# Half tails over the whole array width, and the last batch's fourth product by blocks of tokens

## The chip, the core and the metric

The kernel runs on one core of one Trainium2 chip. The metric is the device time of one execution in microseconds, smaller is better. The kernel before takes 279.53 us (median of three executions, 279.29 to 279.78).

The core's engines each follow their own instruction stream in order. PE multiplies matrices (PEld is its weight load, which runs beside the multiplication), DVE and ACT work elementwise, POOL here only starts DMA loads that convert float32 to bfloat16, and SP starts DMA stores and DMA transposes. PE writes to PSUM, eight banks of 128 partitions by 512 float32 each; DVE and ACT read them.

## The reference

Eight batches of eight heads, 576 tokens, 64 dimensions each: attention in a window of 128 tokens with a linear bias, then a token mixer and a channel MLP on the 512 joined columns.

```
scores = scale * q @ k^T ; bias = -slope[h] * |rel| ; kept where 0 <= rel < 128
x   = softmax(scores + bias) @ v            # [8, 576, 512] with the heads side by side
u   = x + (relu(x^T @ w_tok1) @ w_tok2)^T   # over tokens
out = u + relu(u @ w_ch1) @ w_ch2           # over channels
```

## The kernel before, in words

**Planner.** The kernel does not issue instructions as it walks its loops. Each piece of work is an operation with an engine, a cost in ns, a rank, its inputs and its buffers (`plan.op`, L76). `Plan.run` (L118) plays all of them through on paper: at each step it takes, over all engines, the operation that can start earliest, ties going to the lower rank. `Plan.emit` writes the instructions in the order of the planned starts. So a changed cost can change the order on every engine. Among the costs of PE stands a `mode`: where an operation's mode differs from that of the one before it, the planner adds 95 ns (L267). Random shifts of the ranks have fixed seeds for each batch (L337).

**Stages.** For each batch there is a `side` (L873): attention by blocks of 128 tokens, then the token mixer. And there is a `main` (L993): the channel MLP. The side of batch b+1 is planned to run among the main of batch b. On PE, a block's scores are L670; the exponential on ACT is L693; the multiplication by the window's mask on DVE is L703; the product with V is L736, in two groups of four heads (even heads, odd heads); the division by the row sums is L749 and L752 on DVE (L758 when it falls to ACT). V carries a column of ones, so a product has 65 columns, 64 sums and the row sum.

**Token mixer.** L781 and L791 are its first product, L799 or L800 its ReLU, L824 and L820 its second product, L842 on DVE the addition that gives `ub`. From batch 2 on, SP transposes `ub` by DMA into `uT` (L850); before that PE does it (L859).

**Channel MLP.** L1021 is the first product, in chunks of four matmuls of 512 columns; L1064 is the same for the tail. The second product is a scheme of seven half products in `second` (L1135): products 1, 5, 6, 2, 3, 7, 4 in that order, 12 matmuls of 256 columns each (L1198), in two groups of six. On PE's rows they show by their operands: `WC,r` are products 1 and 2, `WT,s` products 5 and 6, `WC,s` product 3, `WT,r` products 7 and 4. Products 1, 6, 7 and 4 add up in one bank, `g2`, with an addition on DVE (L1169) after each of them. The four finished quarters of the result (256 tokens by 256 columns, 256 KB) go out on SP (L1181), or on POOL in the middle batches. L1109 is the second product of the tail, L1116 its addition, L1126 its store. The last batch has another form of the first product (`unit`, L943 to L987).

**Tails.** 576 tokens are four blocks of 128 and a tail of 64. The tails of two batches share one block of 128 rows, `TAIL`. In the first two pairs (batches 0 to 3; `HALVED`, L345) each batch works out its own half: its 64 tokens are 64 weight columns of the product with V, which land on 64 of PSUM's partitions. In the last two pairs both halves are done at once. A half's operation carries `mode=2`; scores carry `mode=1`.

**End.** The last PE work is product 4 of batch 7, then one addition on DVE of 128 partitions by 512, then one store of 256 KB on SP:

```
L1189  4: (1, 0, True)      # quarter: lower 256 tokens, left 256 columns; last, so it is stored
L1197  first = g == 0 and c == 0 and t == 0 and m not in AFTER
L1198  pe_.matmul(bk()[:, c * HN : (c + 1) * HN], lhsT=l(t, c), rhs=w(t), start=first, ...
```

The 12 matmuls are issued as two groups of six: three of the six steps of the sum for tokens 256 to 383 (`c` = 0) and the same three for tokens 384 to 511 (`c` = 1), then the other three steps of each.

Of the kernel before, what the change touches and what calls it, by code (L numbers as in the profile page):

```python
# [11 lines left out]
ALU = mybir.AluOpType  # L12
# [53 lines left out]
class Plan:  # L66
# [51 lines left out]
    def run(self):  # L118
# [28 lines left out]
        mode, turned = 0, -1e9  # L147
# [53 lines left out]
        def send(o, at, line, work, late):  # L201
            nonlocal flying
            coming.append([at, line, work, o, late])
            flying += 1

        while todo:
            best = None
            for e, c in cand.items():
                pick, early = None, None
                for o in c:  # L210
                    if e == "POOL" and o is not pool[sent]:
                        continue
                    t = max(ready[o], free[e])
# [6 lines left out]
                    for b in o.bufs:  # L220
                        if b.slot is None:
                            got = b.ring.best(b.choice, asked.count(b.choice))
                            asked.append(b.choice)
                            if got is None:
                                t = None
                                break
                            t = max(t, got[0])
                    if t is None:
                        continue
                    if e == "POOL" and len(lanes) >= 8:  # L230
                        if lanes[-8].done is None:
                            continue
                        t = max(t, lanes[-8].done)
# [26 lines left out]
            if e == "PE":  # L260
                slow = 2.0 if t < WARM else 1.0
                if t > free[e] + 1.0:
                    self.gaps.append((free[e], t))
                    if t > free[e] + 3000:
                        slow = 1.6
                    t += 60.0
                elif o.mode != mode:  # L267
                    t += 95.0
                mode = o.mode
                o.t0 = t  # L270
                free[e] = t + o.cost * slow
                o.done = free[e] + 165.0
            elif e == "ACT":
                o.t0, free[e], o.done = t, t + o.cost - 115, t + o.cost
            elif e == "DVE":
                o.t0, free[e], o.done = t, t + max(o.cost - 80, 50), t + o.cost
            elif e == "SP":
                o.t0 = t
                if o.bus:
                    free[e] = t + 1310.0  # L280
                    if o.bus > 1500 and len(turns) > 1:
                        free[e] = max(free[e], turns[-2].done + 1100)
                    turns.append(o)
                    send(o, t + 300, 1, TURN[o.bus > 1500][0], TURN[o.bus > 1500][1])
                else:
                    free[e] = t + 590
                    send(o, t + 300, 1, STORE, 1010.0)
            else:
                o.t0 = t
                free[e] = t + o.cost  # L290
                send(o, t + o.cost, 0, STORE if o.packets < 0 else o.packets * PACKET, 1010.0 if o.packets < 0 else LATE[t > FETCH])
                lanes.append(o)
                sent += 1
# [63 lines left out]
STORE = 774.0  # L357
# [11 lines left out]
def kernel(  # L369
# [15 lines left out]
    nc = tc.nc  # L385
    P = nc.NUM_PARTITIONS
    B, H, S, D = q.shape
    DTOK = moe_w_tok1.shape[1]
    DM = H * D
# [30 lines left out]
    def bank(choice=ONE):  # L420
        return plan.buf("ps", choice)
# [171 lines left out]
    for e in range(2):  # L593
        def go(e=e):
            for i in range(2):
                dve_.tensor_copy(out=maskt[:, e, :, 0, i * R : (i + 1) * R], in_=masks[:, e, :, 0, 0:R])
            dve_.tensor_copy(out=maskt[:, e, :, 1, :], in_=masks[:, e, :, 1, :])
            dve_.memset(maskt[0:R, e, :, 1, R:P], 0.0)
# [112 lines left out]
    def values(pr, blk, half, pb, rank):  # L711
        xb = xbs[pr]
        tail = blk == TAIL
        r0, r1_ = (0, P) if half is None else (half * R, (half + 1) * R)
        vme = held[pr, blk]["v"]
        work = [(r0, r1_, 1, vme)]
        if tail:
            work += [(j * R, (j + 1) * R, 0, held[pr, (j + 1) * NC - 1]["v"]) for j in range(2)
                     if half is None or half == j]
        elif blk % NC:  # L720
            work += [(0, P, 0, held[pr, blk - 1]["v"])]
        both = pr >= PAIRN
        ot = None
        for es in ([[0, 1]] if both else [[0], [1]]):
            n = len(es)
            ot, rt = plan.buf("ps", TWICE) if both else bank(), plan.buf("rt")

            def view(ot=ot, n=n):
                v = ot().rearrange("p (e c) -> p e c", e=n)[:, :, 0 : 4 * (D + 1)]
                return v.rearrange("p e (i d) -> p e i d", i=4)  # L730

            for at, e in enumerate(es):
                def go(e=e, at=at, view=view):
                    mms = [(a, z, kind, vb, i, h) for a, z, kind, vb in work for i, h in enumerate(HEADS[e])]
                    for m, (a, z, kind, vb, i, h) in enumerate(mms):
                        pe_.matmul(view()[a:z, at, i, :], lhsT=pb()[:, e, i, kind, a:z], rhs=vb()[:, h, 0 : D + 1],  # L736
                                   start=m == 0, stop=m == len(mms) - 1, skip_group_check=True)

                rk = rank(240)
                plan.op("PE", 120 * len(work) + (110 if tail and half is None else 0), go, rk,  # L740
                        mode=2 if half is not None else 0, reads=[(pb, e)], uses=[w[3] for w in work],
                        **({"adds": ot} if at else {"makes": ot}))

            def x4(es=es):
                v = xb()[r0:r1_, blk, :].rearrange("p (i e d) -> p e i d", i=4, e=2)
                return v[:, es[0] : es[-1] + 1, :, :]

            def recip(view=view, rt=rt, n=n):
                dve_.reciprocal(out=rt()[r0:r1_, 0:n, :, :], in_=view()[r0:r1_, :, :, D : D + 1])  # L749

            def norm(view=view, rt=rt, n=n, x4=x4):
                dve_.tensor_tensor(out=x4(), in0=view()[r0:r1_, :, :, 0:D],  # L752
                                   in1=rt()[r0:r1_, 0:n, :, :].broadcast_to([r1_ - r0, n, 4, D]), op=ALU.mult)

            def norms(view=view, rt=rt, n=n, x4=x4):
                for e in range(n):
                    for i in range(4):
                        act_.activation(out=x4()[:, e, i, :], in_=view()[r0:r1_, e, i, 0:D], func=ACT.Copy,  # L758
                                        scale=rt()[r0:r1_, e, i, :])

            plan.op("DVE", 180 + 4 * (n - 1), recip, rk, makes=rt, uses=[ot])
            plan.op("DVE", 154 + 270 * n, norm, rk, part=(xb, (blk, half)), uses=[ot, rt],
                    other=("ACT", 115 + 830 * n, norms))
# [370 lines left out]

    def second(b, rank, r2, ss, sums, ub):  # L1135
        pr, half = b // 2, b % 2
        g1, g2, g3 = bank(ANY), bank(ANY), bank(ANY)
        obs = {}
        capt = {}

# [15 lines left out]
        BANK = {1: g2, 6: g2, 7: g2, 4: g2, 2: g1, 5: g3, 3: g3}  # L1156
        AFTER = {6: 1, 7: 6, 4: 7, 3: 5}

        def evict(m, bk, row, col, last):
            key = (row, col)  # L1160
            blks = [half * NC + 2 * row, half * NC + 2 * row + 1]
            cols = slice(col * HN, (col + 1) * HN)
            old = obs.get(key)
            ob = old or obs.setdefault(key, plan.buf("ob"))

            def go():
                v = ob().rearrange("p (c n) -> p c n", c=2)
                src = v if old else ub()[:, blks[0] : blks[0] + 2, cols]
                dve_.tensor_tensor(out=v, in0=bk().rearrange("p (c n) -> p c n", c=2), in1=src, op=ALU.add)  # L1169

            rk = rank(0)
            kw = {"adds": ob} if old else {"makes": ob, "reads": [(ub, x) for x in blks]}
            kw["uses"] = [bk]
            capt[m] = plan.op("DVE", 690, go, rk, **kw)
            if not last:
                return
            late = FROM_P <= b < B - 1
            q_ = nc.gpsimd if late else nc.sync

            def store():  # L1180
                q_.dma_start(out=out[b, row * HS : (row + 1) * HS, cols].rearrange("(c p) n -> p c n", p=P),  # L1181
                             in_=ob().rearrange("p (c n) -> p c n", c=2))

            if late:
                plan.dma(store, 2 * P, -1, uses=ob)
            else:
                plan.op("SP", 550, store, rk, uses=[ob])

        DONE = {1: (0, 0, False), 5: (1, 1, False), 6: (0, 1, False), 7: (1, 1, True), 2: (0, 0, True), 3: (0, 1, True), 4: (1, 0, True)}  # L1189
        for m in PRODUCTS:  # L1190
            l, w, s, tt = L[m]
            bk = BANK[m]
            for g in range(2):
                def go(m=m, g=g, l=l, w=w, bk=bk):
                    for c in range(2):
                        for t in range(3 * g, 3 * g + 3):
                            first = g == 0 and c == 0 and t == 0 and m not in AFTER  # L1197
                            pe_.matmul(bk()[:, c * HN : (c + 1) * HN], lhsT=l(t, c), rhs=w(t), start=first,  # L1198
                                       stop=g == 1 and t == HK - 1, skip_group_check=True)

                rd, needs = [], []
# [14 lines left out]
                if SECOND_LATE and g == 0 and m not in AFTER:  # L1216
                    marks["wait"].append(op)
            evict(m, bk, *DONE[m])

    def along(base, length, total):  # L1220
        done = [0.0]
# [68 lines left out]
```

## Time and profile before

| | us |
|---|---|
| median of three executions | 279.53 |
| the profiled execution, its own time | 280.54 |
| its span, first to last instruction | 278.6 |
| outside of the span | 1.94 |
| PE busy | 271.4 |
| DVE busy | 208.0 |
| ACT busy | 136.0 |
| POOL busy | 116.0 |

The granted clock of PE is 0.997 of full over the span. A line of the timeline reads: start in us from the span's start, duration in us, engine, source line, operation, output<-inputs, the array tile in use (rows*columns), output partitions x columns, and how many instructions were merged into the line; at its end, in brackets, how long the engine had stood idle and what ended that. The duration of a PE line includes the last matmul's way through the array, so the pace is read from start to start. The lines themselves stand in the prediction.

### The profile page before, as it was taken

How to read it: one execution, taken by the hardware profiler on the slowest of the kernel's cores; microseconds unless marked ns; L12 is line 12 of the kernel's file. 1: busy time of each engine (PE TensorE's matmuls, PEld its weight loads, DVE VectorE, ACT ScalarE, POOL GpSimd, SP SyncE). 2: the span in 40 equal slices, each digit the busy share in tenths (PEclk: the TensorE clock that was granted, in tenths of full speed). 3: DMA queues.
4: the chain of work that ended last, by engine and by line, in shares of the span. 5: the costliest groups of instructions: out<-in, count | busy, mean ns of one | idle time of the engine just before them, and what ended most of it. 6: DMA issues, size and time to landing. Idle time of an engine off the chain costs nothing.

```text
span 278.6 us, 6964 instructions
## 1 busy us (share of the span) xinstructions
PE 271.4 (97%) x2825; PEld 180.0 (65%) x2825; DVE 208.0 (75%) x485; ACT 136.0 (49%) x219; POOL 116.0 (42%) x146
## 2 busy tenths in 40 slices
PE   7999999999999999999999999999999999999994
PEld 3664765675686556585567655486667645689883
DVE  7566689978897559862989479673989549876982
ACT  5561885336960189206961097206870079205610
POOL 8999765940256027900486009700472220013000
PEclk9999999999999999999999999999999999999998
DMA  9999999999899999999999979999499750043014
GB/s 133 155 138 152 182 190 192 155 125 203 141 113 100 172 251 123 123 142 180 182 133 158 205 191 88 148 138 240 69 115 99 197 142 2 2 118 129 0 53 137
DMA packets 167535, 38.43 MB, mean 138 GB/s; under 512 B 155792, under 2 KB 166672, under 8 KB 167504
## 3 DMA queue, kind: packets, MB, share of 16 engines
q0 software_dynamic: 116112, 20.03, 92.8%
q1 hardware_dynamic: 50352, 17.70, 32.9%
q8 instruction: 22, 0.36, 0.6%
q10 hardware_dynamic: 1040, 0.26, 0.4%
q14 instruction: 9, 0.07, 0.1%
HBM read 35.85 MB, written 9.44 MB: 163 GB/s over the span
## 4 chain that ended last, share of the span: by engine, by line
PE 85%; DMA 6%; POOL 3%; DVE 2%; issue 1%; ACT 1%; SPq 0%; POOLq 0%
PE ps L1198 25%; PE ps L1021 25%; PE ps L736 6%; PE ps L670 5%; PE ps L824 5%; PE ps L781 5%; PE ps L1064 4%; PE ps L943 3%; PE ps L1109 3%; POOL qk L515 3%; DMA qk<-in_k_dram 2%; DMA qk<-in_q_dram 2%; DMA uT<-ub 1%; PE ps L630 1%; PE ps L791 1%
## 5 line engine op out<-in xcount | busy, mean ns | idle before, releaser
L1021 PE MATMUL ps<-uT,WC 128*128 128x512 bf16 x328 | 79.3, 379 | 0.8 <-DMA uT<-ub 0.7
L693 ACT ACTIVATE pe<-ps 128x1024 bf16<-128x1024 f32 (+1 forms) x76 | 63.4, 888 | 30.4 <-PE ps L670 30.1
L515 POOL DMA_DIRECT2D v<-in_v_dram x40 | 34.0, 860 | 92.8 <-PE ps L736 89.0
L1027 ACT ACTIVATE r<-ps 128x512 bf16<-128x512 f32 x75 | 44.4, 601 | 41.4 <-PE ps L1021 39.6
L1021 PEld LDWEIGHTS <-WC 128*128 128x128 bf16 x328 | 29.1, 98 | 31.1 <-issue 2.3
L703 DVE TENSOR_TENSOR pe<-pe,mask 128x1024 bf16<-128x1024 bf16 (+1 forms) x64 | 38.1, 608 | 9.0 <-ACT pe L693 8.5
L1198 PEld LDWEIGHTS <-r 128*128 128x128 bf16 x384 | 37.1, 98 | 7.3 <-issue 0.2
L515 POOL DMA_DIRECT2D qk<-in_k_dram x39 | 33.8, 873 | 2.9 <-DMA v<-in_v_dram 1.4
L515 POOL DMA_DIRECT2D qk<-in_q_dram x39 | 33.5, 864 | 2.4 <-DMA WC<-in_moe_w_ch_dram 1.3
L1198 PEld LDWEIGHTS <-s 128*128 128x128 bf16 x288 | 27.5, 98 | 5.9 <-issue 1.3
L752 DVE TENSOR_TENSOR xb<-ps,rt 128x256 bf16<-128x256 f32 (+1 forms) x72 | 29.0, 416 | 0.7
L736 PEld LDWEIGHTS <-pe 128*128 128x128 bf16 (+1 forms) x560 | 22.4, 100 | 9.2 <-DVE pe L703 2.1
L736 PE MATMUL ps<-v,pe 128*128 128x65 bf16 (+1 forms) x560 | 26.5, 194 | 0.1
L1198 PE MATMUL ps<-WC,r 128*128 128x256 bf16 x192 | 25.4, 273 | 0.0
L1198 PE MATMUL ps<-WT,s 128*128 128x256 bf16 x192 | 24.6, 273 | 0.0
L1198 PE MATMUL ps<-WT,r 128*128 128x256 bf16 x192 | 23.9, 273 | 0.0
L1169 DVE TENSOR_TENSOR ob<-ps,ub 128x512 f32<-128x512 f32 x22 | 15.0, 685 | 10.3 <-PE ps L1198 10.1
L842 DVE TENSOR_TENSOR ub<-ps,xb 128x512 bf16<-128x512 f32 x34 | 21.2, 681 | 1.9 <-PE ps L824 1.8
L670 PEld LDWEIGHTS <-qkT 64*128 64x128 bf16 x560 | 14.8, 94 | 11.2 <-issue 9.8
L670 PE MATMUL ps<-qkT 64*128 64x128 bf16 (+1 forms) x304 | 19.4, 216 | 0.0
L749 DVE RECIPROCAL rt<-ps 128x4 f32<-128x4 f32 (+1 forms) x76 | 12.4, 175 | 8.8 <-PE ps L736 8.2
L1069 ACT ACTIVATE r2t<-ps 128x512 bf16<-128x512 f32 x12 | 7.2, 602 | 22.5 <-PE ps L1064 22.5
(95 smaller groups left out, 340.1 us busy)
## 6 DMA issues: line engine op xcount, KB each, us to landing
out_dram<-ob SPq DMA_DIRECT2D x17, 256.0 KB, 2.6
v<-in_v_dram POOLq DMA_DIRECT2D x32, 128.0 KB, 5.3
qk<-in_k_dram POOLq DMA_DIRECT2D x31, 128.0 KB, 5.5
qk<-in_q_dram POOLq DMA_DIRECT2D x31, 128.0 KB, 5.0
WC<-in_moe_w_ch_dram POOLq DMA_DIRECT2D x8, 384.0 KB, 9.1
out_dram<-raw SPq DMA_DIRECT2D x7, 256.0 KB, 2.8
out_dram<-ob POOLq DMA_DIRECT2D x5, 256.0 KB, 3.4
out_dram<-raw POOLq DMA_DIRECT2D x3, 256.0 KB, 2.9
```

The source lines that it names most:

```text
L515: nc.gpsimd.dma_start(out=to()[p0 : p0 + n, :, :], in_=rows(src, b, s0, n))
L670: pe_.matmul(wide(e)[:, i, kind, a:z], lhsT=ts[kb]()[e * D : (e + 1) * D, NHP + i, :], rhs=ts[blk]()[e * D : (e + 1) * D, i, a:z], start=n ...
L693: act_.activation(out=pb()[:, e, :, lo:, c0:c1_], in_=wide(e)[:, :, lo:, c0:c1_], func=ACT.Exp, scale=scale)
L703: dve_.tensor_tensor(out=o, in0=o, in1=heads(mk, es), op=ALU.mult)
L736: pe_.matmul(view()[a:z, at, i, :], lhsT=pb()[:, e, i, kind, a:z], rhs=vb()[:, h, 0 : D + 1], start=m == 0, stop=m == len(mms) - 1, skip_g ...
L752: dve_.tensor_tensor(out=x4(), in0=view()[r0:r1_, :, :, 0:D], in1=rt()[r0:r1_, 0:n, :, :].broadcast_to([r1_ - r0, n, 4, D]), op=ALU.mult)
L781: pe_.matmul(t1[j]()[:, :], lhsT=W1[:, c, j * P : (j + 1) * P], rhs=xb()[:, blk, :], start=c == 0, stop=False)
L842: plan.op("DVE", 690, lambda blk=blk, ht=ht, hs=hs: dve_.tensor_tensor(out=ub()[:, blk, :], in0=ht()[:, hs], in1=xb()[:, blk, :], op=ALU.a ...
L1021: pe_.matmul(ct()[:, :], lhsT=WC1[:, cb, t * P : (t + 1) * P], rhs=uT()[:, cb, :], start=cb == 0, stop=cb == NCB - 1)
L1027: plan.op("ACT", 600, lambda t=t, ct=ct: act_.activation(out=r2()[:, t, :], in_=ct()[:, :], func=ACT.Relu), rk, part=(r2, t), uses=[ct], o ...
L1169: dve_.tensor_tensor(out=v, in0=bk().rearrange("p (c n) -> p c n", c=2), in1=src, op=ALU.add)
L1198: pe_.matmul(bk()[:, c * HN : (c + 1) * HN], lhsT=l(t, c), rhs=w(t), start=first, stop=g == 1 and t == HK - 1, skip_group_check=True)
```

## The change

In the planner's cost of a store on SP, a store that is given a smaller cost than 550 takes a smaller share of the queue. Beyond that there are two edits of the work.

First, the half tails' product with V (batches 0 to 3) uses all 128 weight columns and writes all 128 partitions; the 64 rows that are not of this half are never read. The operation loses `mode=2`. The number of matmuls stays the same.

Second, in batch 7 `g2` is a pair of neighbouring banks, the first 256 columns of each in use: tokens 256 to 383 (and 0 to 127) in the one, the others in the second. Product 4 of this batch is issued by `last_product`: six matmuls for tokens 256 to 383, their addition of 128 by 256, a store of 128 KB on SP, and the same for tokens 384 to 511 with the store on ACT's queue.

```diff
@@ Plan.run
-                    send(o, t + 300, 1, STORE, 1010.0)
+                    send(o, t + 300, 1, STORE * o.cost / 550, 1010.0)
@@ values
-                    mms = [(a, z, kind, vb, i, h) for a, z, kind, vb in work for i, h in enumerate(HEADS[e])]
+                    mms = [(0 if half is not None else a, P if half is not None else z, kind, vb, i, h)
+                           for a, z, kind, vb in work for i, h in enumerate(HEADS[e])]
...
                 plan.op("PE", 120 * len(work) + (110 if tail and half is None else 0), go, rk,
-                        mode=2 if half is not None else 0, reads=[(pb, e)], uses=[w[3] for w in work],
+                        reads=[(pb, e)], uses=[w[3] for w in work],
@@ second
-        g1, g2, g3 = bank(ANY), bank(ANY), bank(ANY)
+        final = b == B - 1
+        g1, g2, g3 = bank(ANY), bank(TWO if final else ANY), bank(ANY)
...
+        def of(bk, c):
+            at = c * (DM if final and bk is g2 else HN)
+            return bk()[:, at : at + HN]
+
+        def both(bk):
+            return bk().rearrange("p (c n) -> p c n", c=2)[:, :, 0:HN]
...
-                dve_.tensor_tensor(out=v, in0=bk().rearrange("p (c n) -> p c n", c=2), in1=src, op=ALU.add)
+                dve_.tensor_tensor(out=v, in0=both(bk), in1=src, op=ALU.add)
...
+            if final and m == 4:
+                last_product(b, rank, r2, ub, g2, of, capt[7])
+                continue
...
-                            first = g == 0 and c == 0 and t == 0 and m not in AFTER
-                            pe_.matmul(bk()[:, c * HN : (c + 1) * HN], lhsT=l(t, c), rhs=w(t), start=first,
+                            first = g == 0 and t == 0 and (c == 0 or final and bk is g2) and m not in AFTER
+                            pe_.matmul(of(bk, c), lhsT=l(t, c), rhs=w(t), start=first,
...
+    def last_product(b, rank, r2, ub, g2, of, before):
+        for c in range(2):
+            ob = plan.buf("ob")
+            def go(c=c):
+                for t in range(HK):
+                    pe_.matmul(of(g2, c), lhsT=r2()[:, HK + t, HS + c * P : HS + (c + 1) * P], rhs=WT[:, 3, t, :],
+                               start=False, stop=t == HK - 1, skip_group_check=True)
+            def add(c=c, ob=ob):
+                dve_.tensor_tensor(out=ob()[:, 0:HN], in0=of(g2, c), in1=ub()[:, NC + 2 + c, 0:HN], op=ALU.add)
+            def store(c=c, ob=ob):
+                (nc.sync, nc.scalar)[c].dma_start(out=out[b, HS + c * P : HS + (c + 1) * P, 0:HN], in_=ob()[:, 0:HN])
+            rk = rank(656)
+            plan.op("PE", 656, go, rk, adds=g2, reads=[(r2, HK + t) for t in range(HK)], needs=[lt[0][3], lt[1][3], before])
+            plan.op("DVE", 425, add, rk, makes=ob, uses=[g2], reads=[(ub, NC + 2 + c)])
+            plan.op("SP", 275, store, rk, uses=[ob])
```

**What the planner makes of it.** The order of POOL's instructions is the same. SP's differs in the last store alone, ACT's has one store more at the end. Of PE, DVE and ACT the order differs in the stages of batches 1, 2 and 3; from the main of batch 4 to the last product it is the same again, apart from the banks that are used.

- Side of batch 1 (the before's 38 to 58 us). On PE the order was L736 x8, L781 x3, L736 x8, L781 x3, L1198 x12, L781 x2, L791, L1198 x12, L824. It becomes L736 x8, L1021 x4, L736 x8, L781 x8, L791, L1198 x12, L824; 12 matmuls of L1198 come after L824 instead, and one L1021 chunk stands between the two L736 instead of ahead of both. On DVE the two masks (L703) of the last block stand before the second sum of L1046, not behind it, with one L752 before and one after them. One ReLU of the token mixer goes from ACT to DVE (L800), two copies of `uT` from DVE to ACT.
- Side of batch 2 (78 to 92 us). Six matmuls of L1198 (`WC,r`) from behind L791 change places with six (`WT,s`) from ahead of L781; L781, L791, L824 stay at their places among the work. On DVE L800 stands ahead of the L1169 that was before it.
- Side of batch 3 (105 to 130 us). The two L736 of the last block follow each other, both ahead of a chunk of L1021; six matmuls of L1198 move from before L820 to after L824. The last block but one is divided on DVE, not half of it on ACT; one ReLU goes from ACT to DVE (L800). The first chunk of L1021 of batch 3's main moves ahead of the last 12 matmuls of product 4 of batch 2 and of 16 matmuls of L1064; it needs all four transposes of `uT`.

## The prediction

> **What bounds the kernel now.** I read the page's head and chain first, then the chain in order of time, then PE's timeline with shapes kept apart, whose row at 24.67 us stands last here.
>
> ```profile
> span 278.6 us, 6964 instructions
> PE 271.4 (97%) x2825; PEld 180.0 (65%) x2825; DVE 208.0 (75%) x485; ACT 136.0 (49%) x219; POOL 116.0 (42%) x146
> PE 85%; DMA 6%; POOL 3%; DVE 2%; issue 1%; ACT 1%; SPq 0%; POOLq 0%
> ...
> 24.67 0.40 PE L630 MATMUL ps<-ident,qk 128*128 128x128 bf16 x4 [0.25 <-DMA qk<-in_k_dram]
> ```
>
> The chain that ended last is PE for 85% of the span. Its other pieces lie at the start: up to 24.67 us, the chain in order of time shows, it goes mostly over loads, the last of them a load of k that PE waits for. After that PE works nearly without a break. So an edit pays if it shortens PE's own time after 24.67 us, or the way from PE's last matmul to the end; what it saves before 24.67 us is lost in the wait for that load. The profiled execution took 280.54 us, 1.94 outside its span. It is 1.01 us above the median of the runs, so the sum is made against 280.54 and its difference is taken off 279.53.
>
> **Half tails: the matmuls.** Half and whole width stand side by side in PE's timeline of batch 3's side; the other rows are batches 2 and 1.
>
> ```profile
> 101.89 0.69 PE L736 MATMUL ps<-v,pe 128*64 128x65 bf16 x16
> 102.52 1.90 PE L1021 MATMUL ps<-uT,WC 128*128 128x512 bf16 x8
> ...
> 104.91 0.66 PE L736 MATMUL ps<-v,pe 128*128 128x65 bf16 x16
> 105.40 1.89 PE L1021 MATMUL ps<-uT,WC 128*128 128x512 bf16 x8
> ...
> 78.98 0.69 PE L736 MATMUL ps<-v,pe 128*64 128x65 bf16 x16
> 79.61 0.82 PE L781 MATMUL ps<-xb,W 128*128 128x512 bf16 x3
> ...
> 38.59 1.04 PE L736 MATMUL ps<-v,pe 128*128 128x65 bf16 x24
> 39.57 1.90 PE L1021 MATMUL ps<-uT,WC 128*128 128x512 bf16 x8
> ```
>
> Sixteen half-width matmuls hold PE for 102.52 - 101.89 = 0.63 us, sixteen of whole width for 105.40 - 104.91 = 0.49. Half width saves nothing per matmul, and leaving it costs: 0.14 us in batch 3, and 0.63 - 0.49 = 0.14 in batch 2. In both only the exit counts, since scores stand before it, and PE changes its tile after those either way. In batch 1 eight whole-width matmuls come first: 24 take 0.98, at whole width 24 x 0.49/16 = 0.74, so 0.24. Batch 0's two tails lie before 24.67 us: nothing, covered by the load of k; without that cover they would give some 0.3, two tails of 0.14. These are the direct terms; what the moved order does with them follows.
>
> **Batch 1.** What ended PE's waits here was DVE.
>
> ```profile
> 49.08 0.39 PE L791 MATMUL ps<-xt,W1p 64*128 64x512 bf16 x1
> 49.40 1.48 PE L1198 MATMUL ps<-WC,r 128*128 128x256 bf16 x12
> 50.72 1.46 PE L824 MATMUL ps<-r,W 128*128 128x512 bf16 x6
> ```
>
> ```profile
> 42.46 0.36 DVE L776 COPY xt<-xb 64x512 bf16<-64x512 bf16 x1
> 42.85 0.56 DVE L1046 TENSOR_TENSOR s<-r 128x768 bf16<-128x768 bf16 x1
> 43.44 0.25 DVE L749 RECIPROCAL rt<-ps 128x4 f32<-128x4 f32 x2
> ...
> 44.05 0.75 DVE L752 TENSOR_TENSOR xb<-ps,rt 128x256 bf16<-128x256 f32 x2
> 44.72 1.28 DVE L703 TENSOR_TENSOR pe<-pe,mask 128x1024 bf16<-128x1024 bf16 x2
> ```
>
> The first mask of the last block took half of the 1.28, so it ended near 45.4, and PE's next L736 stood waiting for it. In the new order only L749, one L1046 and one L752 stand between L776 and that mask. From 42.46 I add 0.36 (L776), 0.15 (L749), 0.54 (L1046), 0.39 (L752) and 0.64 (L703), with the gaps between them left out, and come to 44.55. Then PE: L736 8 x 0.031 = 0.24; a chunk of L1021 0.86 (four of 0.216); L736 0.24; L781 8 x 0.22 = 1.73; L791 with its changes of tile 0.32 + 0.10; L1198 x12 1.32 (50.72 - 49.40). That is L824 at 49.36. Before, it was at 50.72 with 12 matmuls of L1198 (1.32) more ahead of it: 49.40 like for like. So the gain is 0.04: DVE sets this, not PE, and most of the half tail's 0.24 is eaten. Ends: 0 (DVE no earlier than worked out), and 0.30 (the 0.24, and what PE loses at the mask); I take 0.10, nearer the worked chain than the row of the matmuls.
>
> **Batch 2.** L781 to L824 keep their places. The stage ends in a wait of PE for `uT`.
>
> ```profile
> 83.18 0.88 POOL L515 DMA_DIRECT2D v<-in_v_dram  x1 [3.30 <-PE ps L736]
> ...
> 88.20 5.56 SPq L850 DMA_TRANSPOSE uT<-ub  x4
> ...
> 96.25 1.89 PE L1021 MATMUL ps<-uT,WC 128*128 128x512 bf16 x8 [0.66 <-DMA uT<-ub]
> ```
>
> The transposes start when L842 is done behind L824 and share the DMA engines with six loads that POOL starts once L736 frees the buffers of V (83.18). Both releases are PE's, so all of it moves with PE: 0.14, and the 0.66 of idling stays. If the transposes don't come earlier, the 0.14 and batch 1's gain are lost here.
>
> **Batch 3.** Here the order does the most.
>
> ```profile
> 110.61 0.68 DVE L703 TENSOR_TENSOR pe<-pe,mask 128x1024 bf16<-128x1024 bf16 x1
> ...
> 117.20 2.47 DVE L842 TENSOR_TENSOR ub<-ps,xb 128x512 bf16<-128x512 f32 x4
> ```
>
> ```profile
> 116.48 0.62 PE L820 MATMUL ps<-r,W2t 128*64 128x512 bf16 x4
> ...
> 124.01 1.95 PE L1064 MATMUL ps<-uTt,WC 128*128 128x128 bf16 x32
> 125.80 1.47 PE L1198 MATMUL ps<-WT,r 128*128 128x256 bf16 x12
> 127.11 1.89 PE L1021 MATMUL ps<-uT,WC 128*128 128x512 bf16 x8
> ```
>
> The last block's second L736 now follows the first at once; its mask, 110.61 to 111.29 before, stands one L752 (0.39) earlier on DVE, so PE, which is there at some 110.8, waits about 0.1 for it, and then as much for the bank that DVE, no longer ACT, has to empty. The gap that PE had ahead of these two falls away, so of the half tail's 0.14 some 0.05 to 0.10 stay. The new wait is that of the moved L1021 chunk for the transposes; behind it on PE queue product 4 of batch 2, all of L1064 but 16 matmuls, and with them DVE's L1169 and ACT's ReLUs.
>
> ```profile
> 119.19 5.17 SPq L850 DMA_TRANSPOSE uT<-ub  x4
> ...
> uT<-ub SPq DMA_TRANSPOSE x1, 2.4
> ```
>
> The last of the four was issued at 119.19 + 5.17 - 1.27 = 123.09 and landed 2.4 later (the answer for the DMA of that stretch alone), at 125.5. PE needs it, from L820: 127.11 - 116.48 = 10.63, less 1.31 (12 of L1198, 127.11 - 125.80) and 0.90 (16 of L1064, half of 125.80 - 124.01), and 0.66 more (six of L1198 that moved behind L824): 9.08 after it. L820 comes 0.66 earlier for those six and some 0.3 for the gains so far: 115.5, so L1021 is reached at 124.6. L842, and with it the transposes, come earlier by the same 0.96 less some 0.05: landing at 124.6. No slack. Bounds of the stall: 0, and 0.9 if the landings stay at 125.5. The loads of POOL that run beside them also start earlier (L736 frees V over a us sooner), so I take 0.1 and put batch 3 at 0.
>
> **The end.** DVE's and SP's last pieces:
>
> ```profile
> 273.25 1.47 PE L1198 MATMUL ps<-WT,r 128*128 128x256 bf16 x12
> 273.45 0.42 DVE L1116 TENSOR_TENSOR raw<-ps,ub 128x256 f32<-128x256 f32 x1 [0.29 <-PE ps L1109]
> 273.94 1.11 SPq L1126 DMA_DIRECT2D out_dram<-raw  x2
> 274.76 0.69 DVE L1169 TENSOR_TENSOR ob<-ps,ub 128x512 f32<-128x512 f32 x1 [0.89 <-PE ps L1198]
> 275.48 0.38 SPq L1181 DMA_DIRECT2D out_dram<-ob  x1
> ```
>
> ```profile
> out_dram<-raw SPq DMA_DIRECT2D x4, 64.0 KB, 2.0
> ...
> out_dram<-ob SPq DMA_DIRECT2D x1, 256.0 KB, 2.2
> ...
> raw<-in_k_dram ACTq DMA_DIRECT2D x1, 256.0 KB, 4.4
> raw<-in_q_dram SPq DMA_DIRECT2D x1, 256.0 KB, 3.8
> ```
>
> The first block's six matmuls end near 273.25 + 0.82 = 274.07 and its addition (0.42, as L1116) at 274.5, hidden by the second six; SP is busy with L1126 until 275.05, then issues. The second addition runs from 274.76 to 275.18 instead of 275.45: 0.27 saved, and its store on ACT's queue waits for nobody. Landing of 128 KB lies between 2.0 (64 KB) and 2.2 us (256 KB, the last store); by bytes 2.07, so 0.13 more. SP's block lands at 275.1 + 2.07 = 277.2, ACT's at 275.2 + 2.07 = 277.3, before 275.48 + 2.2 = 277.7. Term: 0.40. Bounds: 0.50, and -0.20 if a store on ACT's queue is 0.6 later than one on SP's (4.4 against 3.8 at the start, two loads at once, contended). Pairing the banks earlier in batch 7 and the planner's smaller store move no instruction ahead of the last product: nothing.
>
> The Trainium skill, DMA: Bandwidth & Descriptors, Rules for kernel authors, says that two transfers to disjoint partition halves aren't worth it since both spread over the same engines, and that several issuing engines save only issue time. That speaks against this edit; read so, the landing stays 2.2 and the term is 0.27, total 279.02. The 64 KB row at 2.0 leans the other way, by little.
>
> **Sum.** 0.10 + 0.14 + 0 + 0.40 = 0.64: 280.54 becomes 279.90, the median 279.53 becomes 278.89. With every bound good, 0.30 + 0.14 + 0.14 + 0.50 = 1.08, 278.45; with the weak ones, 0 + 0.10 + 0 + 0.27, 279.16.
>
> **Rivals.** (a) The middle is hidden: batch 1's and 2's gain is lost in the wait at 96.25 because the transposes stay DMA-bound. For it: PE's only idling of size is there. Against: their start is PE's. Then the end alone counts: 279.53 - 0.40 = 279.13. (b) Slower: the moved chunk of batch 3 stalls. Batch 2's four transposes took from 88.20 to 96.25, 8.05 us; batch 3's five at that pace, with one more issue of 1.27, take 9.3 from the first issue. That one falls near 117.1 (as L842 starts at 117.20 less 0.96, ends 0.62 later and SP takes some 0.2), so they land at 126.4 and PE stands 1.8 us: 278.89 + 1.7 = 280.6. For it: their DMA engines are shared with POOL's loads in both stages. Against: in batch 3 the five took 7.6 (the first was issued 1.29 ahead of 119.19, at 117.9), and the loads now start sooner. The gain is gone from a stall of 0.74, a landing after 125.3. (c) The store on ACT's queue lands 0.6 late: 278.89 + 0.6 = 279.5. (d) The widened product does not lose its 0.14, because PE's change of tile at its exit has another cause: 278.89 + 0.24 = 279.13; against it, two pairs of rows agree.
>
> **How the numbers follow.** Forecast 0.62, (a) 0.08, (b) 0.18, (c) 0.09, (d) 0.03. A measurement of this kernel tells some 0.2%, 0.56 us, from no change: same is 278.97 to 280.09. The forecast's own range, 278.45 to 279.16, lies for three quarters below 278.97: 0.47; the weaker shapes of (a) and (d), with one bound better than taken, add 0.04: faster 0.51. Of (b), whose stall can be anything from 0.6 to 1.8, 0.14 lies beyond 280.09: slower 0.14. The rest is 0.35. The range, 278.3 to 279.8, holds the forecast's, (a), (c), (d) and the short stalls of (b).
>
> **What would show it.** No `128*64` tile on L736 in batches 1 to 3, and 0.49 us for sixteen. L824 of batch 1 near 49.3; the idle time ahead of batch 2's first L1021 still near 0.66; the first L1021 of batch 3 near 124.7 with little idling, more than 0.6 means (b). From the main of batch 4, everything earlier by one amount, 0.2 to 0.3; two DVE additions of 0.42 at the end, the last store issued 0.3 nearer to the last matmul than before, landing in 2.0 to 2.2. Wrong would be a new idle piece on PE after 130 us, or a landing on ACT's queue above 2.5.

## The result and the profile after

The change made the kernel slower: 280.54 us (median of 22 executions, 279.47 to 281.56) against 279.91 for the kernel before beside it (22 executions), ratio 1.0025 with an interval of 1.0013 to 1.0037. Forecast were 278.89 and a range of 278.3 to 279.8.

The profiled execution of the changed kernel took 280.03 us, its span 277.8. The page's head, its shares of the chain that ended last, and the row of L1022 (L1021 of before; the edit moves lines behind the 734th by one, those of the second product by up to twelve) among the costliest groups:

```profile
span 277.8 us, 6934 instructions
PE 268.9 (97%) x2789; PEld 180.6 (65%) x2825; DVE 208.6 (75%) x486; ACT 135.6 (49%) x216; POOL 115.8 (42%) x146
...
PE 85%; DMA 7%; DVE 3%; issue 2%; ACT 2%; POOL 1%; SPq 0%; DVEq 0%; ACTq 0%
...
L1022 PE MATMUL ps<-uT,WC 128*128 128x512 bf16 x306 | 77.7, 379 | 1.5 <-DMA uT<-ub 0.5
```

PE bounds the kernel as before. Of its 2825 matmuls 2789 have a record, so 2.5 us less of busy time is no gain. The span is 0.8 us shorter in this pair of profiles, and yet the medians say 0.63 us slower: one profile a side doesn't decide here, and the stages have to be compared one by one. PE's timeline, at the places shown of before:

```profile
38.30 0.90 PE L737 MATMUL ps<-v,pe 128*128 128x65 bf16 x24
39.04 1.89 PE L1022 MATMUL ps<-uT,WC 128*128 128x512 bf16 x7
...
41.89 0.66 PE L737 MATMUL ps<-v,pe 128*128 128x65 bf16 x16 [0.41 <-DVE pe L703]
...
49.31 1.03 PE L825 MATMUL ps<-r,W 128*128 128x512 bf16 x4
...
78.88 0.66 PE L737 MATMUL ps<-v,pe 128*128 128x65 bf16 x16
79.38 0.81 PE L782 MATMUL ps<-xb,W 128*128 128x512 bf16 x2
...
95.28 1.90 PE L1022 MATMUL ps<-uT,WC 128*128 128x512 bf16 x8
...
100.94 0.66 PE L737 MATMUL ps<-v,pe 128*128 128x65 bf16 x16
101.44 1.89 PE L1022 MATMUL ps<-uT,WC 128*128 128x512 bf16 x7
...
114.79 0.62 PE L821 MATMUL ps<-r,W2t 128*64 128x512 bf16 x4
...
122.97 1.06 PE L1065 MATMUL ps<-uTt,WC 128*128 128x128 bf16 x16
124.56 1.02 PE L1022 MATMUL ps<-uT,WC 128*128 128x512 bf16 x3 [0.53 <-DMA uT<-ub]
125.42 1.47 PE L1210 MATMUL ps<-WT,r 128*128 128x256 bf16 x12
126.73 1.89 PE L1022 MATMUL ps<-uT,WC 128*128 128x512 bf16 x8
...
272.72 1.47 PE L1239 MATMUL ps<-WT,r 128*128 128x256 bf16 x12
```

Read it against the rows of before, start by start. The half tails now take 0.50 us for sixteen (79.38 - 78.88, 101.44 - 100.94) and 0.74 for twenty-four (39.04 - 38.30): the direct gain is there. PE came into batch 1's tail 0.29 us ahead of before (38.30 against 38.59), by luck of the loads at the start, and was 0.10 ahead at L825 (49.31 against 49.40, like for like). It was 0.97 ahead at batch 2's chunk (95.28 against 96.25), where before had stood 0.66 waiting for `uT`, and 0.38 ahead after batch 3's (126.73 against 127.11). The loss between these two is at one place: the moved chunk of L1022 waited for the transposes.

The stages of all traces were compared in this way, each PE instruction with the same one of before's profile. In the table a stage's figure is by how much PE fell behind (+) or drew ahead (-) in it, against before's profile (to some 0.03 us), and the last column is the median against before's beside it. The page rounds the span to 0.1 us, so the way from the last product's start to the span's end is read from a view that gives that stretch in full. It shows start and end, the length, each engine's busy time with its instructions, the granted clock of PE, and the DMA's share and rate; before first, then the changed kernel:

```profile
273.25:278.62 5.37, 1.47 (x14) 1.07 (x11) 1.12 (x2) 0.00 (x0) 0.00 (x0) 0.83 0.43 139
...
272.72:277.75 5.03, 1.48 (x14) 1.08 (x11) 1.27 (x3) 0.00 (x0) 0.00 (x0) 1.00 0.46 149
```

| kernel | batch 1 (38.6 to 57 us) | half tail of batch 2 | wait ahead of batch 2's chunk | batch 3 (97 to 132) | last product's start to the span's end | outside the span, median | median less before's |
|---|---|---|---|---|---|---|---|
| before | 0 | 0 | 0 (waits 0.66) | 0 | 5.37 us | 2.00 | 0 |
| changed kernel | +0.20 | -0.14 | -0.70 | +0.56 | 5.03 | 2.27 | +0.63 |
| e1 last product alone | 0 | 0 | -0.70 | 0 | 5.02 | 2.49 | 0 |
| e2 same, both stores on SP | 0 | 0 | -0.70 | 0 | 5.20 | 2.14 | -0.03 |
| e3 width, old order | -0.07 | -0.14 | -0.70 | -0.03 | as before | 1.95 | -0.05 |
| e4 width, new order | +0.20 | -0.14 | -0.70 | +0.47 | as before | 1.99 | +0.40 |
| e5 e4, chunk put back | +0.19 | -0.14 | -0.69 | -0.08 | as before | 2.00 | -0.05 |
| e6 new order in batch 1 alone | +0.19 | -0.14 | -0.65 | -0.03 | as before | 1.79 | -0.30 |
| e8 width, old order, one store | -0.01 | -0.14 | -0.57 | -0.01 | 5.21 | 2.00 | -0.58 |
| e9 before, last store on ACT | 0 | 0 | -0.69 | 0 | 5.43 | 2.12 | -0.06 |
| e10 changed, chunk back, one store | +0.19 | -0.14 | -0.70 | -0.09 | 5.23 | 2.16 | -0.37 |
| e11 changed, chunk back | +0.20 | -0.14 | -0.70 | -0.08 | 5.00 | 1.80 | -0.46 |
| e12 before, last store split | 0 | 0 | -0.70 | 0 | 5.24 | 2.11 | -0.16 |
| e13 e8 again | -0.07 | -0.14 | -0.68 | -0.01 | 5.21 | 2.01 | -0.66 |

Three things do not belong to the change. The 0.66 us wait in batch 2 is in before's profile alone: kernels whose half tails are as before (e1, e2, e9, e12) don't have it either. And before batch 1 the profiles stand up to 0.8 us apart by luck of the loads, in both directions, with the same instructions. And between 208 and 226 us, where all kernels have the order of before, PE draws ahead of before's profile by 0.14 to 0.17 in most of the traces, the changed kernel's among them, by less in e12 and e13, and falls behind by 0.03 in e6. The stages of the changed kernel that do count add up to 0.20 - 0.14 + 0.56 - 0.35 + 0.27 = +0.54, and the medians say +0.63, with an interval of about 0.36 to 1.04.

### The profile page after: what moved, and what is told of

Its sections match the earlier page's. It is cut to its first block, busy times and chain, and to the rows that moved or that the text cites. A ratio compares the mean times of both kernels' runs of the same rounds, so it can differ in the third digit from the quotient of the medians.

```text
span 277.8 us, 6934 instructions
## 1 busy us (share of the span) xinstructions
PE 268.9 (97%) x2789; PEld 180.6 (65%) x2825; DVE 208.6 (75%) x486; ACT 135.6 (49%) x216; POOL 115.8 (42%) x146
## 4 chain that ended last, share of the span: by engine, by line
PE 85%; DMA 7%; DVE 3%; issue 2%; ACT 2%; POOL 1%; SPq 0%; DVEq 0%; ACTq 0%
PE ps L1210 25%; PE ps L1022 23%; PE ps L737 6%; PE ps L670 6%; DMA WC<-in_moe_w_ch_dram 6%; PE ps L782 4%; PE ps L825 4%; PE ps L1110 4%; PE ps L1065 4%; PE ps L944 3%; PE ps L1287 2%; ACT pe L693 1%; POOL qk L515 1%; PE ps L630 1%; DVE pe L703 1%
## 5 line engine op out<-in xcount | busy, mean ns | idle before, releaser
L1022 PE MATMUL ps<-uT,WC 128*128 128x512 bf16 x306 | 77.7, 379 | 1.5 <-DMA uT<-ub 0.5
L1028 ACT ACTIVATE r<-ps 128x512 bf16<-128x512 f32 x76 | 45.1, 600 | 43.7 <-PE ps L1022 39.8
L1022 PEld LDWEIGHTS <-WC 128*128 128x128 bf16 x328 | 29.1, 97 | 30.1 <-issue 1.5
L703 DVE TENSOR_TENSOR pe<-pe,mask 128x1024 bf16<-128x1024 bf16 (+1 forms) x64 | 38.2, 608 | 8.9 <-ACT pe L693 8.5
L1210 PEld LDWEIGHTS <-r 128*128 128x128 bf16 x372 | 35.8, 98 | 7.1 <-issue 0.2
L1210 PE MATMUL ps<-WT,r 128*128 128x256 bf16 x180 | 22.4, 273 | 0.0
L1178 DVE TENSOR_TENSOR ob<-ps,ub 128x512 f32<-128x512 f32 x21 | 14.3, 685 | 8.5 <-PE ps L1210 8.3
```

The lines of the kernel that those rows point to most:

```text
L703: dve_.tensor_tensor(out=o, in0=o, in1=heads(mk, es), op=ALU.mult)
L1022: pe_.matmul(ct()[:, :], lhsT=WC1[:, cb, t * P : (t + 1) * P], rhs=uT()[:, cb, :], start=cb == 0, stop=cb == NCB - 1)
L1028: plan.op("ACT", 600, lambda t=t, ct=ct: act_.activation(out=r2()[:, t, :], in_=ct()[:, :], func=ACT.Relu), rk, part=(r2, t), uses=[ct], o ...
L1178: dve_.tensor_tensor(out=v, in0=both(bk), in1=src, op=ALU.add)
L1210: pe_.matmul(of(bk, c), lhsT=l(t, c), rhs=w(t), start=first, stop=g == 1 and t == HK - 1, skip_group_check=True)
```

## The experiments

All kernels here compute the whole result. Each was run twelve times beside 35 executions of before.

### First four: which edit, and which part of it

e1 takes the last product of the changed kernel alone. e2 is e1 with one line changed:

```diff
-                (nc.sync, nc.scalar)[c].dma_start(out=out[b, HS + c * P : HS + (c + 1) * P, 0:HN], in_=ob()[:, 0:HN])
+                nc.sync.dma_start(out=out[b, HS + c * P : HS + (c + 1) * P, 0:HN], in_=ob()[:, 0:HN])
```

e3 takes the half tails' whole width alone and leaves the planner its mode, so that the order stays that of before; e4 takes the whole edit of the half tails.

```diff
+                    mms = [(0 if half is not None else a, P if half is not None else z, kind, vb, i, h)
...
-                        mode=2 if half is not None else 0, reads=[(pb, e)], uses=[w[3] for w in work],   # e4 alone
+                        reads=[(pb, e)], uses=[w[3] for w in work],
```

> Only the last product's edit (two banks, two additions, a store on SP and one on ACT's queue); the tails stay at half width, so the order of all other instructions is the before's. Theory: the way from the last product's first matmul to the last landing is 0.37 us shorter, but a store at the end on ACT's queue adds 0.3 us outside of the span (1.94 becomes 2.25), so the time falls by only 0.1. Rival: what lies outside of the span has nothing to do with ACT's store; it stays at 1.94 and the time falls by 0.4.

> As the last product's edit alone, but both short stores on SP. Theory (ACT's queue costs outside of the span): outside 1.94 again; the second store is issued some 0.5 us after the first, so the span is 0.1 to 0.2 shorter than before and the time falls by as much. Rival: outside stays at 2.25 although no store is on ACT's queue.

> Half tails at whole width, but the planner still counts a change of mode, so the order of all instructions is the before's; the last product as before. Theory (the moved order is what costs): PE gains 0.14 us in batches 2 and 3 and up to 0.24 in batch 1, no new wait, time 0.2 to 0.5 lower, outside 1.94. Rival (the whole width itself costs): time the same or higher.

> Half tails at whole width with the order that the planner then makes (the changed kernel's), the last product as before. Theory: the first chunk of batch 3's channel MLP waits 0.4 to 0.9 us for the transposes, batch 1 gains nothing; time 0.2 to 0.6 higher than before, outside 1.94. Rival (only the end makes the changed kernel slower): time 0.2 to 0.3 lower.

Measured: e1 0.9996 (0.9976 to 1.0016), e2 1.0000 (0.9984 to 1.0016), e3 0.9989 (0.9970 to 1.0008), e4 1.0013 (0.9998 to 1.0028). The ratios are not quotients of the table's medians; for e3 the two differ by 0.1%. By times alone only e4 leans to slower, as expected, and its interval just holds 1. The others missed their expectations: e1 won 0.35 us of span, as its theory had it, but had 0.49 more outside of it, e2 won 0.17 and had 0.14 more outside, which is neither its theory nor its rival, and e3 was to be 0.2 to 0.5 faster. e4's profile says where it loses; PE's timeline of e4 and the same place in e3:

```profile
122.58 1.06 PE L1065 MATMUL ps<-uTt,WC 128*128 128x128 bf16 x16
124.07 1.02 PE L1022 MATMUL ps<-uT,WC 128*128 128x512 bf16 x3 [0.43 <-DMA uT<-ub]
124.93 1.47 PE L1199 MATMUL ps<-WT,r 128*128 128x256 bf16 x12
126.24 1.89 PE L1022 MATMUL ps<-uT,WC 128*128 128x512 bf16 x8
```

```profile
37.90 0.90 PE L737 MATMUL ps<-v,pe 128*128 128x65 bf16 x24
38.64 1.89 PE L1022 MATMUL ps<-uT,WC 128*128 128x512 bf16 x7
...
41.32 0.66 PE L737 MATMUL ps<-v,pe 128*128 128x65 bf16 x16 [0.24 <-DVE pe L703]
```

e4 has the same stall as the changed kernel. The sixteen L1065 end 0.90 after their start, at 123.48, so PE stands 0.59 until 124.07. e3 shows batch 1: twenty-four products take 0.74 us instead of 0.98, and 3 us later PE waits 0.24 for DVE's mask, as much as it had won. So the width gives at most 0.07 in batch 1 (the table), even in the old order. In batch 3 e3 wins the tail's 0.14 at 102 us and by 108 us only 0.03 of it is left.

### Second four: batch 3 or batch 1, and the stores

e5 is e4 with batch 3's first chunk behind batch 2's fourth product again. On PE sixteen matmuls of the token tail change places with the four of the chunk; ACT's ReLUs follow, DVE, POOL and SP keep their order.

```diff
-                plan.op("PE", 862, go, rk, makes=ct, reads=[(uT, x) for x in blocks if x != TAIL], needs=[lc1[t]])
+                plan.op("PE", 862, go, rk, makes=ct, reads=[(uT, x) for x in blocks if x != TAIL], needs=[lc1[t]],
+                        behind=[marks["p", 2, 4]] if b == 3 else [])
...
+            marks["p", b, m] = op          # in second, after each product
```

e6 gives the changed order to batch 1 alone (`mode=2` stays in the other batches). e8 is e3 with the last product of the changed kernel, its two additions into one buffer and one store of 256 KB on SP. e9 is before with `nc.scalar` for its last store.

> Half tails at whole width with the changed kernel's order, last product as before, and one thing moved: batch 3's first chunk of its channel product (four matmuls, PE) stands behind batch 2's fourth product again and sixteen matmuls of the token tail fill its place. If the chunk's wait for the transposes is what the order costs: no idle piece ahead of batch 3's first chunk, and 0.4 to 0.7 us less than the same kernel without the move, so 0.9985 to 1.000 of before. If the order of batch 1 costs it instead: the same 0.3 to 0.4 us above before as without the move, ratio 1.001 to 1.0015, with the stall gone and nothing gained. If the stall only moves (PE then waits somewhere behind): ratio as without the move, and a new idle piece of 0.4 or more between the token tail and batch 3's main.

> Half tails at whole width; the order is that of before except in batch 1, which has the changed kernel's order. Last product as before. If batch 3's chunk is the whole loss: the same as with the width alone, ratio 0.9985 to 1.0. If batch 1's order costs some 0.26 us (what its stretch lost in the profile of the tails' edit against that of the width alone): ratio 1.000 to 1.001, and PE's offset to the width-only kernel changes by 0.2 to 0.3 us between 41 and 62 us. My prediction had this order as a gain of 0.10 with bounds 0 and 0.30.

> Half tails at whole width in the order of before; batch 7's last product by blocks of tokens in two banks with two short additions, but one store of 256 KB on SP's queue, as before. If each store or queue at the end has a price outside the span (0.14 for a second store on SP, 0.3 to 0.5 for a last store on ACT's queue), this kernel pays none: time outside the span 1.9 to 2.1 us, the span 0.27 shorter than with the width alone, and a time 0.2 to 0.4 us below before, ratio 0.9985 to 0.9993. If the difference outside the span comes with the last product's new form and not with its stores: 2.14 or more outside the span, ratio 0.9995 to 1.0005.

> The kernel before with one thing changed: its last store (256 KB) is issued on ACT's queue, not SP's. If ACT's queue at the end costs time outside the span: 2.3 to 2.5 us outside it instead of 2.0, the span the same or up to 0.2 shorter (ACT waits for nobody), ratio 1.0 to 1.002. If not: 1.9 to 2.1 outside the span.

Measured: e5 1.0002 (0.9989 to 1.0015), e6 0.9990 (0.9967 to 1.0014), e8 0.9977 (0.9957 to 0.9998), e9 0.9997 (0.9984 to 1.0010). e5's profile has no idle piece at the chunk, and batch 3 goes from +0.47 in e4 to -0.08; no wait takes its place behind it. The medians move by 0.45 the same way, but the two intervals overlap, so here the traces decide. e6 loses 0.26 us in batch 1 against the width alone (+0.19 against e3's -0.07), within the 0.2 to 0.3 expected (0.20 against e8, which has the old order too); its time doesn't show it, since it had only 1.79 us outside the span. e8 came out faster than expected, though its last product won 0.17 of span and not 0.27. e9 has 2.12 outside the span, at the edge of the 1.9 to 2.1 expected without a price and far from 2.3 to 2.5. So the price of 0.3 to 0.5 that e1 and the changed kernel seemed to show is not ACT's queue.

### Last four: the change mended

e11 is the changed kernel with e5's edit, e10 is e11 with one store as in e8, e12 is before with its last store cut in two, one on SP and one on ACT, and e13 is e8 once more.

> The changed kernel with batch 3's first chunk put back behind batch 2's fourth product, nothing else. If the chunk's wait is most of what the change lost: no idle piece of 0.3 or more ahead of batch 3's first chunk, 0.4 to 0.7 us less than the changed kernel, ratio to before 0.9995 to 1.0010 instead of 1.0025. If the loss lies in the end (time outside the span) and batch 1: ratio still 1.0015 or more. Time outside the span as in the changed kernel, 2.2 to 2.5.

> The same, and the last product's two blocks go out in one store of 256 KB on SP's queue. If the two stores cost what the time outside the span suggests (0.27 in the changed kernel) and one store loses little of the end's gain: outside the span 1.8 to 2.1, 0.1 to 0.3 us less than with the two stores, ratio 0.9985 to 1.0005. If the time outside the span has nothing to do with the stores: the same outside as with two, and a span longer by 0.1. What is left against the kernel with the order of before is batch 1's order, some 0.2 us.

> The kernel before with one thing changed: its last store goes out as two of 128 KB, one on SP's queue and one on ACT's. If two stores on two queues are what costs time outside the span: 2.3 to 2.5 outside it, and a ratio of 1.000 to 1.002. If it is the rest of the program's form: 1.9 to 2.1 outside the span, and 0 to 0.2 gained in it, ratio 0.999 to 1.0.

> The kernel with whole-width half tails in the order of before, the last product in two banks and one store, once more. If it really beats before: ratio 0.997 to 0.9993, outside the span 1.9 to 2.1. If the first measurement was luck of the start: 0.9995 to 1.0005.

Measured: e11 0.9978 (0.9961 to 0.9995), e10 0.9981 (0.9964 to 0.9999), e12 0.9996 (0.9980 to 1.0012), e13 0.9982 (0.9963 to 1.0001). PE's timeline and SP's queue of e11:

```profile
123.02 1.95 PE L1065 MATMUL ps<-uTt,WC 128*128 128x128 bf16 x32
124.81 1.47 PE L1210 MATMUL ps<-WT,r 128*128 128x256 bf16 x12
126.11 1.89 PE L1022 MATMUL ps<-uT,WC 128*128 128x512 bf16 x7
```

```profile
116.24 1.94 SPq L851 DMA_TRANSPOSE uTt<-ub  x1
118.27 5.14 SPq L851 DMA_TRANSPOSE uT<-ub  x4
```

The five transposes take as long to issue as in the changed kernel (7.17 us, from 116.24 to 123.41), and PE doesn't notice: by the time it reaches the first chunk, 1.3 us of product 4 and 0.9 us of the token tail have passed. This one move takes the changed kernel from 0.63 us above before to 0.46 below, with intervals that don't meet. Of these 1.09 us the traces show 0.64 in batch 3 (+0.56 to -0.08). The expectation said 0.4 to 0.7; the rest is more than it allowed for, and 0.47 of it (2.27 to 1.80) lies outside the span, where its forecast of 2.2 to 2.5 failed: the stores at the end are the same in both. e12 and e10, too, have 2.1 outside, with two stores and with one. So what lies outside the span does not follow the stores.

e11, measured once, and e8 beat both kernels. e8's repetition gives the same ratio within 0.0005, with an interval that just reaches 1. Between the two the runs don't decide, and the stages don't either: e11 pays 0.20 us for batch 1's order and wins 0.37 at the end, e8 pays nothing and wins 0.17.

## Why the prediction was wrong, point by point

**The stall in batch 3: the step that failed.** "L842, and with it the transposes, come earlier by the same 0.96 less some 0.05: landing at 124.6. No slack." and, from it, "I take 0.1 and put batch 3 at 0". PE's half of this step held: the chunk was to be reached 9.08 us after the token mixer's second product of the tail, and it was, at 122.97 + 0.90 = 123.87, which is 9.08 after 114.79. The other half did not. The timeline of POOL and of SP's queue, of the changed kernel and then of before:

```profile
111.25 0.90 POOL L515 DMA_DIRECT2D v<-in_v_dram  x1
...
116.20 1.86 SPq L851 DMA_TRANSPOSE uTt<-ub  x1
118.15 5.16 SPq L851 DMA_TRANSPOSE uT<-ub  x4
```

```profile
112.76 0.88 POOL L515 DMA_DIRECT2D v<-in_v_dram  x1 [0.52 <-PE ps L736]
...
117.90 1.19 SPq L850 DMA_TRANSPOSE uTt<-ub  x1
```

The first transposition goes out 1.41 us after L821 (116.20 - 114.79), just as before (117.90 - 116.48 = 1.42). But the five issues then take 7.11 us (to 123.31) instead of 6.46 (117.90 to 124.36), and `uT` arrives when PE starts, at 124.56: 9.77 after L821, where I had 9.1. So PE stood 0.69 us. I had moved the landing with its start and kept its duration, which left a slack of zero, and then priced the stall at 0.1 with bounds of 0 and 0.9; the sum's weak end left even that 0.9 out and carried batch 3 as 0. The five traces with the new order in batch 3 give 6.96 (e4) to 7.18 (e10) for the five issues, the nine of the old order 6.44 to 6.54. The extra lies in a single issue, the first or the second of the five: it takes 1.76 to 1.95 us (1.86 in the row at 116.20), where none in the old order takes more than 1.31. Why it takes longer is not shown. In the new order POOL's loads, which share the DMA engines, go out without a break there (the row at 111.25), where before they waited 0.52 us for L736 (112.76). This holds for all five traces against all nine, but the order of PE moves both, and no run changed the loads alone.

This was rival (b), with a sign of its own ("more than 0.6 means (b)"): right in its place and mechanism, its price of up to 1.8 too high, and its chance of 0.18 too low for a step without slack. Its point of decision, a stall of 0.74 us, lay on gains that weren't all there: with batch 1 going the other way 0.69 was enough.

**Batch 1: a term with the wrong sign.** Forecast was a gain of 0.10 with 0 as its worse bound; six traces of the new order lose 0.19 or 0.20, and whole width in the old order gains 0.01 to 0.07. DVE's rows of the changed kernel:

```profile
38.82 0.43 DVE L750 RECIPROCAL rt<-ps 128x4 f32<-128x4 f32 x2
39.28 0.42 DVE L753 TENSOR_TENSOR xb<-ps,rt 128x256 bf16<-128x256 f32 x1
39.74 0.19 DVE L750 RECIPROCAL rt<-ps 64x4 f32<-64x4 f32 x1
39.96 0.69 DVE L703 TENSOR_TENSOR pe<-pe,mask 128x1024 bf16<-128x1024 bf16 x1
...
42.33 0.29 DVE L777 COPY xt<-xb 64x512 bf16<-64x512 bf16 x1
```

and the same rows of before:

```profile
39.12 0.18 DVE L749 RECIPROCAL rt<-ps 128x4 f32<-128x4 f32 x1
39.34 0.42 DVE L752 TENSOR_TENSOR xb<-ps,rt 128x256 bf16<-128x256 f32 x1
39.79 0.27 DVE L749 RECIPROCAL rt<-ps 64x4 f32<-64x4 f32 x2
40.09 0.69 DVE L703 TENSOR_TENSOR pe<-pe,mask 128x1024 bf16<-128x1024 bf16 x1
```

The chain that I had worked out from L776 was right, and so was its end: L825 forecast at 49.36, measured at 49.31. Wrong was what it stood on. I took L776's start of 42.46 out of before's profile as it was. PE came into this stage 0.29 ahead of that profile, and in the old order such a lead is kept (e1, e2, e9, e12: 0). Here L777 started only 0.13 ahead. In the new order the half tail's first reciprocal stands before the last full block's division, and from the first of these rows to the mask DVE takes 1.14 us (39.96 - 38.82) instead of 0.97 (40.09 - 39.12), so the masks come 0.17 late. PE, which had won 0.24, waits 0.41 for the second of them (the row at 41.89), and 0.41 - 0.24 = 0.17 is most of the loss. I had looked at DVE's order behind L776 and not ahead of it.

**Batch 2: right.** Sixteen products in 0.50 us, 0.14 gained, in all nine traces with whole width. Rival (d) falls with it. The idle 0.66 that was to stay behind it is gone, not by the change: it was an accident of the one profile that I had, and the sum had been made against an execution that held it. Rival (a) has no wait left to hide in.

**The end: right in the span, and not in the time.** Forecast were 0.40, two additions of 0.42 and a last store issued 0.3 nearer. DVE's rows, and the landings of the last microseconds (stores, KB each, median us from issue to landing):

```profile
273.58 0.42 DVE L1243 TENSOR_TENSOR ob<-ps,ub 128x256 f32<-128x256 f32 x1 [0.23 <-PE ps L1239]
274.24 0.42 DVE L1243 TENSOR_TENSOR ob<-ps,ub 128x256 f32<-128x256 f32 x1 [0.23 <-PE ps L1239]
```

```profile
out_dram<-ob SPq DMA_DIRECT2D x1, 128.0 KB, 2.1
out_dram<-ob ACTq DMA_DIRECT2D x1, 128.0 KB, 1.8
```

From the last product's start to the span's end it is 0.35 us less (5.37 to 5.03; 0.37 in e11), close to the 0.40. SP's store is now the last to land, not ACT's: its issue takes longer, 0.54 us against the 0.38 of before.

```profile
273.41 1.11 SPq L1127 DMA_DIRECT2D out_dram<-raw  x2
274.62 0.54 SPq L1246 DMA_DIRECT2D out_dram<-ob  x1
```

Rival (c) falls: ACT's store landed after 1.8 us, not late. Of the gain two short additions are 0.17 (e8, with one store; e2, with two on SP, has no more), and two stores on two queues the other 0.18. A split store without the rest gives 0.13 of span (e12), the 0.13 that I had by bytes; its time, ratio 0.9996 (0.9980 to 1.0012), is too coarse to show it. The Trainium skill, DMA: Bandwidth & Descriptors, Rules for kernel authors, advises against two transfers to disjoint partition halves, since both spread over the same engines. e12's trace speaks for the bytes and not for that reading: the two halves landed 1.7 and 2.0 us after their issue, the whole store in before after 2.2. Each store here spans all 128 partitions, so that row of the page is near this case and not on it.

**What no step of mine held:** the time outside the span, 2.27 us in the changed kernel against 2.00. I had assumed the 1.94 of before's profile to stay.

Summed up, forecast against measured: batch 1 -0.10 and +0.20, batch 2 -0.14 and -0.14, batch 3 0 and +0.56, the end -0.40 and -0.35, outside the span 0 and +0.27.

## What to carry to other kernels

When an edit changes a planner's costs, look for the instruction that moved ahead of a transfer it needs: a step with no slack by your own numbers should be forecast as a stall, since a transfer's duration moves too when its neighbours do. Putting one such piece back behind work that needs nothing new can be worth more than the edit itself. Compare stages, by the same instruction in both traces, and check with a second profile that a wait you build on is there every time.

## What was not expected of the hardware

The time outside the span looks like a property of each built kernel, and it doesn't follow what the kernel does at its end. Over the executions of one kernel it stays close to its median (e1 2.45 to 2.55, the changed kernel 2.23 to 2.35, before, the widest, 1.72 to 2.17), e8 gives 2.00 and e13, the same kernel later, 2.01, and before has a median of 2.00, 2.02 and 2.00 on three chips. Between kernels it goes from 1.79 (e6) to 2.49 (e1). The changed kernel and e11 differ in the place of one chunk on PE and in the order of ACT's ReLUs behind it, 150 us ahead of the end, and by 0.47 us outside of the span. What sets it was not tried. It is as large as most terms of this study: 0.47 us are 0.17% of the time.
